# A third score slot from two idle PSUM banks in the w_out stages of a fused attention and squared-ReLU MLP kernel

## The chip, the cores and the metric

The kernel runs on one core of one Trainium2 chip. The metric is device time in microseconds (us). Before the change the median of 11 runs is 370.78 us (370.6 to 372.24).

## What is computed

Attention without a softmax, over 8 batches of 12 heads, 448 tokens and 64 features a head, and then an MLP over the 3584 tokens:

```python
scores = scale * np.matmul(q, k.transpose(0, 1, 3, 2))
attn = np.maximum(scores, 0.0) ** 2 / S
x = np.matmul(attn, v)            # heads side by side: 3584 x 768
g = np.maximum(x @ w_in, 0.0) ** 2    # w_in 768 x 2048
out = g @ w_out                   # w_out 2048 x 768
```

Inputs and outputs are float32 in device memory; on the chip the operands are float16 and the sums float32 in PSUM.

## The kernel before

**Attention.** A unit is four heads of one batch: 24 units, three to a batch. Each unit is cut into 7 tiles of 64 keys. `score` (L252) makes one tile: four matmuls on 64x64 quarters of the array (L262), whose 448 columns go to two PSUM banks, and one ScalarE activation over both banks (L266, relu, 128x896) that writes the tile `at` to SBUF. VectorE then squares `at` in place (L369, queued by `square`). When a unit's seven tiles are squared, `av_unit` (L301) multiplies them with v: 28 quarter-array matmuls (L317) into two banks, and one activation (L323) that writes `xt`.

**A visit** (`visit`, L371) is what the kernel puts between two matmuls of the MLP: a first score tile, then attn x v of a unit if one is due, then a second score tile. Below, S2 is a visit of two tiles, SAS one of two tiles with attn x v between them. Both kinds take their PSUM from a pool of two slots of two banks each (`slot`, L195).

**The MLP** takes the other four banks, which two pools of two banks hold (`big`, handed out by `mm_tile`). Batches 0 and 1 go through `h_group` (plain matmuls, L409), the later ones through `h_period` (L538): 14 products of 6 matmuls, by a Strassen-like scheme that makes 7 block products do the work of 8. The w_out stage (`o_groups`) does the same for two rows of 128 tokens at a time, which is called a group here: seven products, numbered k = 0 to 6 as in its table `products`, of 8 matmuls each (L725). Two banks X and Y collect them. After k = 0, 2, 4 and 5 ScalarE copies X out (`copy`, L627, "m1", "u2", "u3"; at k = 5 L675), and since the later products go on adding to the same bank, k = 4 cannot begin before the copy "u2" of k = 2 is done, nor k = 5 before the copy "u3" of k = 4. VectorE adds the copies to Y (`plus`, L632), and makes the sums of `g` that serve as left operands (`sums`, L594): sum 3 has to be there before k = 4, sum 4 before k = 6. Group n uses the pool n % 2; the first product of group n + 1 stands between k = 4 and k = 5 of group n.

**The order** is written out by hand. The matmuls of the MLP form one list of steps with costs; a clock adds up the costs, and events (visits, prefetches, sums) are put in at steps marked as edges once their time has come. For each pair of batches from the second on, 21 visits of two tiles are spread evenly in time over the w_out stage of the pair before and the first half of its own w_in stage. Between products a visit has to stand on a step with edge set; a k = 5 edge may take one up to 1.6 us early. VectorE's squares wait in queues (`due`, `due_g`), which `fill` and `put` empty by a modelled time; `sums` puts every square that is ready within 0.3 us ahead of the sum. There are four w_out stages, for batch pairs 0 to 3, with 3, 4, 3 and 4 groups; the last has no visits left.

Of the kernel before, what the change touches and what calls it, by code (L numbers as in the profile page):

```python
# [12 lines left out]
FP32 = mybir.dt.float32  # L13
AF = mybir.ActivationFunctionType
# [4 lines left out]
def kernel(  # L19
# [9 lines left out]
    nc = tc.nc  # L29

    B, H, S, D = q.shape
    NT, DM = out.shape
# [11 lines left out]
    J = 7  # L44
    PW = S // J
    NU = 3
    NUN = B * NU
# [7 lines left out]
    SK = 256.0  # L55
    CX = 1.0 / 896.0
# [137 lines left out]
    def slot(dtype, third=False):  # L194
        return (third_p if third else s_p).tile(  # L195
            [P, 2, 2048 // mybir.dt.size(dtype)], dtype, name="slot", tag="slot")
# [54 lines left out]
    now = [0]  # L251
    avt = [None]  # L252

    def score(t, times=1, third=False):
        n, j = divmod(t, J)
        qT, kT = qkt[n]
        ps = slot(FP32, third)
        for hh in list(range(2)) * times:
            r = slice(64 * hh, 64 * hh + 64)
            for hp in range(2):  # L260
                c = slice(64 * hp, 64 * hp + 64)
                nc.tensor.matmul(  # L262
                    ps[c, hh, 0:S], lhsT=kT[r, j, c], rhs=qT[r, :, c],
                    start=True, stop=True)
        at = at_p.tile([P, 2, S], FP16, name="at", tag="at")
        nc.scalar.activation(out=at, in_=ps[:, :, 0:S], func=AF.Relu, scale=SK)  # L266
        ats[t] = at
        seen[t] = now[0]

# [28 lines left out]

    unit = [NU]

    def av_unit():  # L301

        n = unit[0]
        if n == NUN or seen.get(n * J + J - 1, 10 ** 6) >= now[0]:
            return
        unit[0] += 1
        flush(rest=False)
        at_pe[0] += 1.33
        b, u = divmod(n, NU)
        vt = vts[n]  # L310
        ps = slot(FP32)
        for j in range(J):
            at = ats.pop(n * J + j)
            for hp in range(2):
                r = slice(64 * hp, 64 * hp + 64)
                for hh in range(2):
                    nc.tensor.matmul(  # L317
                        ps[64 * hh:64 * hh + 64, hp, 0:S],
                        lhsT=vt[r, hh, j * D:(j + 1) * D], rhs=at[r, hh, :],
                        start=(j == 0), stop=(j == J - 1))  # L320
        if u == 0:
            xts[b] = x_p.tile([P, NM, S], FP16, name="xt", tag="xt")
        nc.scalar.activation(  # L323
            out=xts[b][:, 2 * u:2 * u + 2, :], in_=ps[:, :, 0:S],
            func=AF.Copy, scale=CX)

    def prefetch(m):
        if m >= NUN:
            return
        dma_transpose(m)  # L330
        if m > NPE:
            load_v(m)
        if m + 2 < NUN:
            load_qk(m + 2)
# [7 lines left out]
    at_pe = [0.0]  # L342
    at_ve = [0.0]

    def flush(rest=True):
        for d in (due, due_g) if rest else (due,):
            while d:
                put(d)

    def put(d):  # L350
        ready, cost, fn, _ = d.popleft()
        at_ve[0] = max(at_ve[0], at_pe[0], ready) + cost
        fn()

    def fill(until):
        for d in (due, due_g):
            while d and max(at_ve[0], at_pe[0], d[0][0]) + d[0][1] <= until:
                put(d)

    def now_ve(cost, lag=0.25):  # L360
        at_ve[0] = max(at_ve[0], at_pe[0] + lag) + cost
# [5 lines left out]
    def square(at, lag=0.0):  # L367
        due.append((at_pe[0] + lag, 0.54,
                    lambda: nc.vector.tensor_mul(at, at, at), 0))  # L369

    def visit(tiles):  # L371
        now[0] += 1
        for t in tiles:
            if t % J == 0 and t >= NPE * J:
                prefetch(t // J + 2)
        for t in tiles[:1]:
            score(t)
        av_unit()
        for t in tiles[1:]:
            score(t)  # L380
        at_pe[0] += 0.19 + 0.19 * len(tiles)
        for i, t in enumerate(tiles):
            square(ats[t], 0.6 + 0.85 * i)
# [5 lines left out]
    def mm_tile(i=None, dtype=FP32):  # L389
        if i is None:  # L390
            mm_no[0] += 1
            i = mm_no[0] % len(big)
        return big[i].tile(
            [P, 2048 // mybir.dt.size(dtype)], dtype, name="mm", tag="mm")
# [174 lines left out]
    def tile_of(row):  # L569

        if row in saved:
            return saved[row]
        pr, tb = row
        assert not due_g or due_g[0][3] > 2 * pr + (tb >= 3)
        return gts[pr][:, :, tb * P:(tb + 1) * P]
# [8 lines left out]
    def sums(i, rows, to):  # L584

        a1, a2 = tile_of(rows[0]), tile_of(rows[1])
        x, y = ((a2[:, LO], a2[:, HI]), (to.get(1), a1[:, LO]),
                (a1[:, LO], a2[:, LO]), (a1[:, HI], to.get(2)))[i - 1]
        to[i] = late["s"].tile([P, KH, P], FP16, name=f"s{i}", tag=f"s{i}")
        op = nc.vector.tensor_add if i == 1 else nc.vector.tensor_sub  # L590
        while due and due[0][0] <= max(at_ve[0], at_pe[0]) + 0.3:
            put(due)
        now_ve(0.6)
        op(to[i], x, y)  # L594

    def o_groups(groups, then):
# [5 lines left out]
        def group(n, rows, last):  # L602
# [7 lines left out]
            def needs(k):  # L610

                return max(2 * p + (tb > 2) for p, tb in groups[k]
                           if (p, tb) not in saved)

            def ahead(i, k=n):
                if k < len(groups) and i not in sets[k]:
                    flush_g(needs(k))
                    sums(i, groups[k], sets[k])
# [95 lines left out]
            def step(k, f):  # L714
                acc, fresh, left, right, end = products[k]
                if last and k == 5:
                    acc, fresh = Z, True

                def run():
                    if f == 0 and fresh and k != 3:  # L720
                        acc[:] = [mm_tile((n + (k == 5)) % 2)]
                    if f == 0 and k == 0:
                        ahead(1)
                        ahead(2)
                    nc.tensor.matmul(  # L725
                        acc[0][:, 0:HALF], lhsT=left()[:, f], rhs=right[:, f],
                        start=(fresh and f == 0),
                        stop=(f == KH - 1), skip_group_check=not fresh)
                    if f == KH - 1:
                        end()  # L730
                        if k < 4 and n + 1 < len(groups):
                            some = sum(d[3] <= needs(n + 1) for d in due_g)
                            for _ in range(-(-some // (4 - k))):
                                put(due_g)
                        fill(at_pe[0] + AFTER[k])
                return run

            ls = [[(0.1625, step(k, f), ((2 if k == 5 else True) if f == 0 else False))
                   for f in range(KH)] for k in range(7)]
            if last:  # L740
                ls[6] = [(0.0825, step3(z, f), False) for z in range(2) for f in range(KH)]
# [2 lines left out]
        def pre(i):  # L744
            sums(i, groups[0], sets[0])

        lists = [group(n, rows, rows == LAST) for n, rows in enumerate(groups)]
        for n, ls in enumerate(lists):
            for k in range(7):
# [26 lines left out]
    NB0 = NU * J  # L776
    ps = slot(FP32, True)
# [3 lines left out]
    def s(t, times=2):  # L781
        score(t, times, third=t in THIRD)
# [103 lines left out]
    events = []  # L886
    seq = [[2, 3], 4, [4, 5], [6, 7], [8, 9], 5, [10, 11], [12, 13], [14, 15],
           [16, 17], [18, 19], [20], []]
    for i, ts in enumerate(seq):
        at = (2.5 + i) * T_G  # L890
# [18 lines left out]
    for m in (6, 7):  # L909
        events.append((T_H + (1 + 3 * (m - 6)) * T_G, lambda m=m: prefetch(m)))  # L910
    at0 = T_H + 8 * T_G
    for pr in range(1, B // 2):
        t0 = 2 * NB0 * pr
        end = begin[pr] + T_S - 6.5
        gap = (end - at0) / 21
        for i in range(21):
            ts = [t0 + 2 * i, t0 + 2 * i + 1]
            events.append((at0 + i * gap, lambda ts=ts: visit(ts), True))
        at0 = end
        for i in range(4):  # L920
            events.append((begin[pr] - 6 + i, lambda b=2 * pr, i=i: sums_x(b, i)))
    events.append((at0 + 0.3, lambda: visit([]), True))

    def pre(pr, i):
        def run():
# [29 lines left out]
                steps += periods[b, i0]  # L955
        steps += outs[pr][0]

    clock, last = 0.0, 0.0
    ev = deque(sorted(events, key=lambda e: e[0]))
    for cost, fn, edge in steps:  # L960
        fired = 0
        while ev and edge and ev[0][0] <= clock + (1.6 if edge == 2 and not fired else 1e-3):
            if len(ev[0]) == 3:
                if clock < last + 1.5:
                    break
                last = clock
            ev.popleft()[1]()
            fired += 1
        if fn is not None:
            at_pe[0] += cost  # L970
            fn()
        clock += cost
# [31 lines left out]
```

## Time and profile before

| | |
|---|---|
| median of 11 runs | 370.78 us |
| the profiled execution's own time | 370.75 us |
| its span in the profile | 369.0 us |
| TensorE (PE) busy | 359.9 us, 98% |
| VectorE (DVE), ScalarE (ACT) busy | 265.7 us (72%), 247.5 us (67%) |
| granted TensorE clock | 0.999 |

The span is the profile's first to last instruction; 1.75 us of the execution lie outside of it. "Busy" counts the union of an engine's instructions. A row of the timeline gives start, length, engine, line, operation, destination and source; "x8" means eight instructions merged. "PEld" is the loading of weights, which runs beside the matmuls, and "SPq" a DMA queue. In the chain of waits each row is a stretch of the work that ended last, by what held it.

### The profile page before, as it was taken

The page shows a single profiled execution, that of the slowest core. Times are in us where ns is not written, and L with a number is a line of the kernel's source. Part 1 is how long each engine was busy: PE and PEld are TensorE (multiplying, and loading weights), DVE is VectorE, ACT ScalarE, POOL GpSimd, SP SyncE. Part 2 cuts the span into 40 slices and gives each one's busy share as a digit, 9 for nine tenths or more (in the row PEclk, how much of TensorE's full clock was granted, in tenths as well). Part 3 has the DMA queues.
Part 4 walks back from the last instruction along what each step waited for, and adds up shares of the span by engine and source line. Part 5 has one row for each costly group of instructions (what it writes and reads, how often), then busy time and mean ns, then how long its engine had stood idle before and what let it go on. Part 6 is the DMA issues. An engine that isn't in the chain of part 4 may idle for free.

```text
span 369.0 us, 8720 instructions
## 1 busy us (share of the span) xinstructions
PE 359.9 (98%) x3588; PEld 230.5 (62%) x3588; DVE 265.7 (72%) x470; ACT 247.5 (67%) x371; POOL 107.1 (29%) x128
## 2 busy tenths in 40 slices
PE   8899999999999999999999999999999999999994
PEld 3644445445455778875555588786555689986663
DVE  2997677996777787788585766989766686884442
ACT  3988894787676999876556588887665885532220
POOL 8545521846553155432135045140000000000001
PEclk9999999999999999999999999999999999999999
DMA  7999999999999999998699899692323300003333
GB/s 115 202 204 205 205 204 163 148 162 157 195 164 133 175 98 91 110 111 67 138 161 108 163 155 88 89 115 38 64 73 88 85 3 2 2 0 84 88 90 83
DMA packets 121158, 42.63 MB, mean 116 GB/s; under 512 B 100832, under 2 KB 117760, under 8 KB 121120
## 3 DMA queue, kind: packets, MB, share of 16 engines
q0 software_dynamic: 82912, 23.01, 61.9%
q1 hardware_dynamic: 38048, 18.98, 26.0%
q8 instruction: 28, 0.46, 0.5%
q10 hardware_dynamic: 160, 0.10, 0.1%
q14 instruction: 10, 0.08, 0.1%
HBM read 45.61 MB, written 11.01 MB: 153 GB/s over the span
## 4 chain that ended last, share of the span: by engine, by line
PE 90%; ACT 3%; DVE 3%; issue 1%; DMA 1%; POOLq 0%; POOL 0%; ACTq 0%
PE mm L725 34%; PE mm L538 27%; PE slot L262 10%; PE mm L409 9%; PE slot L317 7%; ACT at L266 3%; DMA q<-in_q_dram 1%; DVE at L297 1%; PE avt L280 1%; PE slot L238 1%; PE mm L238 0%; DVE at L369 0%; PE slot L210 0%; DVE xt L292 0%; ACT u L627 0%
## 5 line engine op out<-in xcount | busy, mean ns | idle before, releaser
L266 ACT ACTIVATE at<-slot 128x896 f16<-128x896 f32 x168 | 145.8, 925 | 22.2 <-PE slot L262 22.2
L369 DVE TENSOR_TENSOR at<-at 128x896 f16<-128x896 f16 x147 | 87.3, 620 | 9.7 <-ACT at L266 9.6
L109 POOL DMA_DIRECT2D qs<-in_q_dram x36 | 35.3, 983 | 114.7 <-DMA qT<-qs 106.9
L725 PEld LDWEIGHTS <-s 128*128 128x128 f16 x440 | 41.5, 98 | 32.7 <-issue 3.6
L262 PE MATMUL slot<-qT,kT 64*64 64x448 f16 x744 | 56.8, 361 | 1.9 <-ACT at L266 1.4
L538 PEld LDWEIGHTS <-w 128*128 128x128 f16 x576 | 54.3, 98 | 5.1 <-issue 4.3
L538 PE MATMUL mm<-xt,w 128*128 128x224 f16 x432 | 48.9, 259 | 0.0
L725 PEld LDWEIGHTS <-g 128*128 128x128 f16 x336 | 31.7, 98 | 24.1 <-issue 4.7
L538 PEld LDWEIGHTS <-ws 128*128 128x128 f16 x432 | 40.3, 98 | 4.7 <-issue 4.7
L632 DVE SCALAR_TENSOR_TENSOR osb<-mm,u 128x384 f32<-128x384 f32 (+1 forms) x30 | 16.2, 543 | 36.4 <-ACT u L627 24.0
L725 PE MATMUL mm<-b,g 128*128 128x384 f16 x224 | 40.7, 326 | 0.0
L725 PE MATMUL mm<-b,s 128*128 128x384 f16 x216 | 39.6, 326 | 0.2 <-DVE s L594 0.2
L409 PE MATMUL mm<-xt,w 128*128 128x448 f16 x192 | 39.8, 354 | 0.0
L725 PE MATMUL mm<-t,s 128*128 128x384 f16 x224 | 39.3, 326 | 0.0
L109 POOL DMA_DIRECT2D ks<-in_k_dram x36 | 35.1, 976 | 8.9 <-DMA b<-in_moe_w_out_dram 5.9
L262 PEld LDWEIGHTS <-kT 64*64 64x64 f16 x744 | 19.0, 104 | 28.7 <-issue 23.3
L561 POOL DMA_DIRECT2D out_dram<-osb x2 | 1.1, 563 | 119.6 <-DVE osb L632 119.6
L627 ACT ACTIVATE u<-mm 128x384 f32<-128x384 f32 x28 | 13.7, 491 | 31.6 <-PE mm L725 27.1
L538 PE MATMUL mm<-x,ws 128*128 128x224 f16 x288 | 34.1, 259 | 0.0
L481 DVE CUSTOM_DVE_ANT_0 g<-mm,m 128x448 f16<-128x448 f32 x36 | 22.4, 624 | 14.9 <-PE mm L538 8.1
L317 PE MATMUL slot<-at,vt 64*64 64x448 f16 x588 | 31.9, 350 | 0.2 <-DVE at L369 0.2
L409 PEld LDWEIGHTS <-w 128*128 128x128 f16 x192 | 17.1, 98 | 19.2 <-issue 5.1
(76 smaller groups left out, 401.0 us busy)
## 6 DMA issues: line engine op xcount, KB each, us to landing
out_dram<-osb SPq DMA_DIRECT2D x52, 192.0 KB, 2.9
vt<-in_v_dram POOLq DMA_DIRECT2D x24, 224.0 KB, 6.1
qs<-in_q_dram POOLq DMA_DIRECT2D x36, 112.0 KB, 4.3
ks<-in_k_dram POOLq DMA_DIRECT2D x36, 112.0 KB, 5.5
w<-in_moe_w_in_dram POOLq DMA_DIRECT2D x8, 384.0 KB, 12.0
b<-in_moe_w_out_dram POOLq DMA_DIRECT2D x4, 768.0 KB, 17.2
q<-in_q_dram POOLq DMA_DIRECT2D x6, 224.0 KB, 7.4
k<-in_k_dram POOLq DMA_DIRECT2D x6, 224.0 KB, 7.8
```

Source lines behind the costliest of these rows:

```text
L109: nc.gpsimd.dma_start(out=t[:, :, hh, :], in_=heads(src, n)[:, hh].rearrange("p (j d) -> p j d", d=D))
L238: nc.tensor.transpose(pss[i][64 * hh:64 * hh + 64, i if n < 4 else 0, j * P:(j + 1) * P], src[:, hh, j * D:(j + 1) * D], ident)
L262: nc.tensor.matmul(ps[c, hh, 0:S], lhsT=kT[r, j, c], rhs=qT[r, :, c], start=True, stop=True)
L266: nc.scalar.activation(out=at, in_=ps[:, :, 0:S], func=AF.Relu, scale=SK)
L317: nc.tensor.matmul(ps[64 * hh:64 * hh + 64, hp, 0:S], lhsT=vt[r, hh, j * D:(j + 1) * D], rhs=at[r, hh, :], start=(j == 0), stop=(j == J - 1))
L369: lambda: nc.vector.tensor_mul(at, at, at), 0))
L409: nc.tensor.matmul(cell[0][:, 0:S], lhsT=w1[f // 4][:, m, (f % 4) * P:(f % 4 + 1) * P], rhs=xts[b][:, m, :], start=(m == 0), stop=(m == NM ...
L481: nc.vector._custom_dve(TENSOR_ADD_SAT, out=gs(s, hi, right), in0=acc(s, y), in1=keep[s, nm], s0=3.4e38, s1=0.0)
L538: nc.tensor.matmul(XY[s][y][:, r * Q:(r + 1) * Q], lhsT=left(k, i0 + 2 * s + r, m), rhs=right(k, m), start=(fresh and r == 0 and m == 0), ...
L627: nc.scalar.activation(out=t, in_=X[0][:, 0:HALF], func=AF.Copy, scale=CO)
L632: nc.vector.scalar_tensor_tensor(out=osb[row][:, c], in0=acc[0][:, 0:cc.stop - cc.start], scalar=CO, in1=keep[nm][:, cc], op0=ALU.mult, op ...
L725: nc.tensor.matmul(acc[0][:, 0:HALF], lhsT=left()[:, f], rhs=right[:, f], start=(fresh and f == 0), stop=(f == KH - 1), skip_group_check=n ...
```

## The change

Visits in w_out stages may have three tiles. The first tile, or attn x v if it is due, then takes two banks of the pool that the current group does not use (`ps=pair[0]`), one bank for each half, and its result is taken out by two activations of 448 columns, one a bank, where the old slot took one of 896. Edges that allow it: the one before k = 2 in every group (three tiles, attn x v or not), and the one before k = 4 in all but the last group of a stage (three tiles, or two without the spare banks if attn x v is due at the next visit). The plan is now a line of tiles against time, which a visit may run ahead of by 1.5 tiles on the named edges and on k = 5. `sums` no longer puts all ready squares first: only those that would be done 0.5 us (sum 3) or 0.9 us (the others) from now on TensorE's clock.

```diff
-    def score(t, times=1, third=False):
+    def score(t, times=1, third=False, ps=None):
...
-        ps = slot(FP32, third)
+        spare = ps is not None
+        ps = slot(FP32, third) if ps is None else [mm_tile(ps), mm_tile(ps)]
...
-        nc.scalar.activation(out=at, in_=ps[:, :, 0:S], func=AF.Relu, scale=SK)
+        if spare:
+            for hh in range(2):
+                nc.scalar.activation(
+                    out=at[:, hh], in_=ps[hh][:, 0:S], func=AF.Relu, scale=SK)
+        else:
+            nc.scalar.activation(out=at, in_=ps[:, :, 0:S], func=AF.Relu, scale=SK)
...
+    def av_due(more=0):
         n = unit[0]
-        if n == NUN or seen.get(n * J + J - 1, 10 ** 6) >= now[0]:
+        return n < NUN and seen.get(n * J + J - 1, 10 ** 6) < now[0] + more
...
-    def visit(tiles):
+    def visit(tiles, spare=None):
...
         for t in tiles[:1]:
-            score(t)
-        av_unit()
+            score(t, ps=None if av_due() else spare)
+        av_unit(spare)
...
-        while due and due[0][0] <= max(at_ve[0], at_pe[0]) + 0.3:
-            put(due)
+        fill(at_pe[0] + (0.5 if i == 3 else 0.9))
         now_ve(0.6)
         op(to[i], x, y)
...
-            ls = [[(0.1625, step(k, f), ((2 if k == 5 else True) if f == 0 else False))
+            free = (n + 1) % 2
+            edges = {2: (free, 3, 3)} if n == len(groups) - 1 else {
+                2: (free, 3, 3), 4: (free, 3, 2)}
+            ls = [[(0.1625, step(k, f),
+                    ((edges.get(k), k == 5) if f == 0 else False))
                    for f in range(KH)] for k in range(7)]
...
+            elif pair is not None and ahead <= 1.5 and clock > last + 1.25:
+                n = min(pair[1 + av_due(1)], NT - tile_no)
+                visit(list(range(tile_no, tile_no + n)), pair[0] if n == 3 else None)
+                tile_no += n
+                last = clock
+            elif ahead <= (1.5 if soon else 0.0) and clock > last + 1.5:
+                n = min(2, NT - tile_no)
+                visit(list(range(tile_no, tile_no + n)))
+                tile_no += n
+                last = clock
```

The number of matmuls, tiles, sums, squares and DMAs is the same as before. `av_unit` with `spare` takes its two banks out with two activations in the same way as `score`.

More of the change, by code (lines that the diff above doesn't have):

```diff
@@ L262, in score @@
                 nc.tensor.matmul(
-                    ps[c, hh, 0:S], lhsT=kT[r, j, c], rhs=qT[r, :, c],
+                    ps[hh][c, 0:S] if spare else ps[c, hh, 0:S],
+                    lhsT=kT[r, j, c], rhs=qT[r, :, c],
                     start=True, stop=True)
         at = at_p.tile([P, 2, S], FP16, name="at", tag="at")
-        nc.scalar.activation(out=at, in_=ps[:, :, 0:S], func=AF.Relu, scale=SK)
+        if spare:
[4 more added lines that the diff above has]
+            nc.scalar.activation(out=at, in_=ps[:, :, 0:S], func=AF.Relu, scale=SK)
         ats[t] = at
@@ L299, with av_unit @@
     unit = [NU]
-    def av_unit():
+    def av_due(more=0):
         n = unit[0]
-        if n == NUN or seen.get(n * J + J - 1, 10 ** 6) >= now[0]:
+        return n < NUN and seen.get(n * J + J - 1, 10 ** 6) < now[0] + more
+    def av_unit(ps=None):
+        if not av_due():
             return
+        n = unit[0]
         unit[0] += 1
@@ L310, in av_unit @@
         vt = vts[n]
-        ps = slot(FP32)
+        spare = ps is not None
+        ps = [mm_tile(ps), mm_tile(ps)] if spare else slot(FP32)
         for j in range(J):
@@ L317, in av_unit @@
                     nc.tensor.matmul(
-                        ps[64 * hh:64 * hh + 64, hp, 0:S],
+                        ps[hp][64 * hh:64 * hh + 64, 0:S] if spare
+                        else ps[64 * hh:64 * hh + 64, hp, 0:S],
                         lhsT=vt[r, hh, j * D:(j + 1) * D], rhs=at[r, hh, :],
@@ L322, in av_unit @@
             xts[b] = x_p.tile([P, NM, S], FP16, name="xt", tag="xt")
+        if spare:
+            for hp in range(2):
+                nc.scalar.activation(
+                    out=xts[b][:, 2 * u + hp], in_=ps[hp][:, 0:S],
+                    func=AF.Copy, scale=CX)
+            return
         nc.scalar.activation(
@@ L911 @@
     at0 = T_H + 8 * T_G
+    plan: list = []
     for pr in range(1, B // 2):
@@ L914 @@
         end = begin[pr] + T_S - 6.5
[L915 to L918, printed above, removed]
+        plan.append((at0, end, t0))
         at0 = end
@@ L921 @@
             events.append((begin[pr] - 6 + i, lambda b=2 * pr, i=i: sums_x(b, i)))
-    events.append((at0 + 0.3, lambda: visit([]), True))
     def pre(pr, i):
@@ L956, with planned @@
         steps += outs[pr][0]
-    clock, last = 0.0, 0.0
+    def planned(t):
+        n = 0.0
+        for a, e, t0 in plan:
+            if t >= a:
+                n = t0 + min(1.0, (t - a) / (e - a)) * 2 * NB0
+        return n
+    clock, last, tile_no = 0.0, 0.0, 2 * NB0
+    NT = NUN * J
     ev = deque(sorted(events, key=lambda e: e[0]))
     for cost, fn, edge in steps:
[L961 to L965, printed above, removed]
-                last = clock
-            ev.popleft()[1]()
-            fired += 1
+        while ev and edge and ev[0][0] <= clock + 1e-3:
+            ev.popleft()[1]()
+        if edge and clock >= plan[0][0]:
+            pair, soon = edge if edge is not True else (None, False)
+            ahead = tile_no - planned(clock)
+            if tile_no == NT:
+                if unit[0] < NUN and clock > last + 1.5:
+                    visit([])
+                    last = clock
[3 more added lines that the diff above has]
+                tile_no += n
+                last = clock
+            elif ahead <= (1.5 if soon else 0.0) and clock > last + 1.5:
[3 more added lines that the diff above has]
+                last = clock
         if fn is not None:
```

## The prediction

> **What bounds the kernel now.** I read the page first, then the chain of waits by line, then the timeline stage by stage. The page:
>
> ```profile
> PE 359.9 (98%) x3588; PEld 230.5 (62%) x3588; DVE 265.7 (72%) x470; ACT 247.5 (67%) x371; POOL 107.1 (29%) x128
> ...
> PE 90%; ACT 3%; DVE 3%; issue 1%; DMA 1%; POOLq 0%; POOL 0%; ACTq 0%
> ```
>
> TensorE is busy 98% of the span and 90% of the chain that ended last. So no other engine is the bound; time can be won only where TensorE loses some between matmuls, or where it waits for ACT or DVE. Both can be read from the timeline of TensorE in the first w_out stage:
>
> ```profile
> 83.08 0.57 PE L262 MATMUL slot<-qT,kT 64*64 64x448 f16 x8
> 83.59 2.77 PE L725 MATMUL mm<-t,s 128*128 128x384 f16 x16
> 86.29 0.57 PE L262 MATMUL slot<-qT,kT 64*64 64x448 f16 x8
> 86.80 1.47 PE L725 MATMUL mm<-b,s 128*128 128x384 f16 x8
> 88.11 1.46 PE L725 MATMUL mm<-b,g 128*128 128x384 f16 x8
> 89.50 0.38 PE L262 MATMUL slot<-qT,kT 64*64 64x448 f16 x4
> ```
>
> Starts are the numbers to use, since ends are modelled. From 86.80 to 88.11 a product takes 1.31 us (1.304 over many). From visit to visit, 83.08 to 86.29, is 3.21. Two products are 2.61. Eight score matmuls are worth 0.37, because four run side by side and a tile adds 0.187 (attn x v, 28 of the same, is 1.32 in the chain). That leaves 3.21 - 2.61 - 0.37 = 0.23 us for going into and out of the quarter-array matmuls. I made this sum for all visits from 67 to 304 us, in w_out and w_in stages, with and without attn x v: 0.22 to 0.25 in nearly all. So **a visit has a fixed price of 0.23 us**, whatever it holds.
>
> Six intervals are longer, by these waits: 0.46 at 113.9, 0.17 at 127.0, 0.36 at 202.0, 0.22 at 285.2, and several of 0.06. Together they are 1.4 us. The cause of the one at 285.2 is in the chain of waits, and it will be needed again:
>
> ```profile
> 285.64 1.60 ACT at L266 x2
> 287.24 0.04 issue
> 287.28 0.50 ACT u L627
> 287.78 0.04 issue
> 287.82 1.46 PE mm L725 x8
> ```
>
> A visit started at 285.20. ACT took its two tiles out from 285.64, and only then, 2.08 us after the visit's start, began the copy u3 of X, which had to end before k = 5 could write X, at 287.82. A short w_in piece of 0.57 us was all that lay between, and TensorE stood for 0.22 us. At 202.0 it is sum 3, late behind squares:
>
> ```profile
> 204.15 0.63 DVE L369 TENSOR_TENSOR at<-at 128x896 f16<-128x896 f16 x1 [0.18 <-ACT at L266]
> 204.69 0.68 DVE L594 TENSOR_TENSOR s<-g 128x1024 f16<-128x1024 f16 x1
> ...
> 205.43 0.34 PE L725 MATMUL mm<-b,s 128*128 128x384 f16 x1 [0.20 <-DVE s L594]
> ```
>
> DVE waited for ACT to make the square's tile, and the sum stood behind it. At 113.9 attn x v waited for a square, behind a `plus` that itself waited for u3.
>
> **Part 1: fewer visits.** I counted the runs of quarter-array matmuls in the two programs' order on TensorE: 88 before, 82 after. All matmuls are the same in number. 6 x 0.23 = **-1.4 us**. The fixed price does not grow with a third tile: the third adds 0.187, as the second does, and these are only moved.
>
> **Part 2: the old waits.** The three in w_out stages, 0.46 + 0.36 + 0.22 = 1.04, all lie in the last group of their stage, where the change rearranges everything. In the new order sum 3 stands ahead of the visit's squares and by the rows' durations is done 0.9 to 2 us before k = 4; the visit before k = 4 that pushed back u3 is gone; and attn x v finds the `plus` further ahead. **-1.0 us.** At 127.0 an attn x v visit followed 24 w_in matmuls after another one with two relus of w_in ahead on ACT; after the change the visits there stand at other places: **-0.2**. If they return, this costs nothing beyond the term. What comes next in these places is part 3.
>
> **Part 3: what the third tile does to ACT.** ACT takes the spare tile out in two halves. No spare eviction exists before; the nearest rows are the relus of w_in, of the same size:
>
> ```profile
> 125.25 1.72 ACT L266 ACTIVATE at<-slot 128x896 f16<-128x896 f32 x2
> 126.84 1.00 ACT L490 ACTIVATE g<-mm 128x448 f16<-128x448 f32 x2
> 127.69 0.97 ACT L266 ACTIVATE at<-slot 128x896 f16<-128x896 f32 x1
> ```
>
> Two full tiles hold ACT from 125.25 to 126.84, 0.80 each (0.82 elsewhere), two halves from 126.84 to 127.69, 0.85. So the third tile puts the next copy back by 0.85 to 0.91 us; I take 0.88, while TensorE gets only 0.19 us more to do. ACT's own extra work, 13 x 0.06 us for thirteen split evictions, is off the path, since ACT is busy 67%.
>
> A rule of the Trainium skill speaks against the change. The page "ScalarE: Activation LUTs", section "Rules for kernel authors", budgets about 0.3 us for each ACTIVATE and 0.83 ns for an element. By it two halves would cost 1.34 us where one full tile costs 1.04, a third tile would delay the copy by 1.34 and the waits of the next paragraph would be near 0.65 us each, 5.2 in all, and the kernel slower than before. The rows above speak against it: 0.85 for two halves beside 0.80 for one tile.
>
> Now the place. A three-tile visit before k = 2 starts at 0. Products go on at 0.69, k = 2 and k = 3 take 2.61, so k = 4 is due at 3.30. ACT starts the copy u2 at 2.08 + 0.88 = 2.96 and k = 4 can start 0.54 later (287.28 to 287.82), at 3.50: a wait of **0.2 us** (0.17 to 0.23). With two tiles it was ready at 2.62, due at 3.11, with 0.5 us to spare, which is why before shows no such wait. Where another visit stands before k = 4 (0.6 us or more) the wait is covered; where none does, it is paid. The same holds for a three-tile visit before k = 4 with no visit before k = 5: u3 at 3.50, k = 5 due at 0.69 + two products = 3.30. In the changed order I count thirteen visits of three tiles. Five are covered; eight are not: in the first stage the one of the last group, in the second stage those of groups 0, 2 and 3 before k = 2 and of group 1 before k = 4, in the third stage group 0 before k = 4 and groups 1 and 2 before k = 2. 8 x 0.19 = **+1.5 us**. From both sides: 0 if ACT gets to the halves early (the first needs only half a tile's matmuls, all four of which run at once, so at most a few hundredths), 8 x 0.46, the longest wait seen, if more is queued: 3.7. I take 1.5, by the nearest row.
>
> **Part 4: the spare banks.** They are those of group n - 1, so the first half waits for the last copy of X there, the second for the `plus` of k = 6 on DVE. This is a new wait, and behind it on TensorE stands everything. In the row of DVE after the attn x v visit at 89.50, the last square ends at 93.76 and the `plus` starts at 94.14. In the new order one more square (0.55) comes before it, and the `plus` of u3 leaves 0.7 us later, since ACT has a third tile ahead of u3. So it ends near 89.50 + 6.0, and the visit comes at 89.50 + 5.83: **+0.2 us**, once. At the other twelve I find the `plus` done 0.1 us or more ahead. Bounds: none (nothing if DVE is 0.2 us earlier), 13 x 0.2 = 2.6.
>
> **Part 5: nothing.** DMA: the transposes of q and k, in the same order on SP, land in 4.5 us (median) and are used two units, some 20 us, later; the first stage draws tiles faster (1.5 us a tile for 1.8) and leaves that cover. No queue of SP or POOL changes its order. If that cover were gone, a unit's first visit would wait; no score matmul waits for a transpose now. The squares moved behind sums 1, 2 and 4 cost nothing as long as attn x v comes later than they do, which is rival 2.
>
> **Sum**, against the profiled execution's 370.75 (span 369.0 and 1.75 outside): 370.75 - 1.4 - 1.0 - 0.2 + 1.5 + 0.2 = **369.9 us**. The median of the runs is 370.78, so both bases are one. A measurement of this kernel can tell about 0.2%, 0.74 us, from no change: 370.04 and below is faster, 371.52 and above slower. The forecast lies 0.1 us beyond the edge.
>
> **Rival 1: the copies do not wait.** If ACT takes halves out sooner than I read, or slack arises elsewhere, the eight waits of part 3 go. Half of them gone: 369.1; all: 368.4. For it: the margin is 0.2 us of 3.5. Against: the same sum gives 287.82 for the wait at 285.2 to the hundredth.
>
> **Rival 2: attn x v waits for squares, and the kernel is slower.** The mechanism is that of 113.9: DVE is in order, the `plus` of u3 waits for ACT, and squares stand behind it. The place is the attn x v visit that follows a three-tile visit holding its unit's last tile: I find four (first stage in groups 0 and 1 and at its end, second stage at its end). In the first of them I get the square done 0.07 us before its matmul, so one more DVE instruction (0.55) decides. Price: the 0.46 us seen once, four times: 369.9 + 1.8 = 371.7; with a further square each, 373.9. It decides from 1.6 us in all, 0.4 a place. Against: in three of the four the sum gives 0.5 us or more to spare, and sums ahead of squares are only two at a time.
>
> **Rival 3: the change doesn't do what it says**, and the two effects cancel: waits of 0.3 instead of 0.19 give 370.8, no change.
>
> **Chances.** The forecast with its own range 369.3 to 370.5: 0.62, half of it below the 0.2% edge. Rival 1: 0.21, faster. Rival 2: 0.12, slower. Rival 3: 0.05. So faster 0.31 + 0.21 = 0.52, within 0.2% 0.31 + 0.05 = 0.36, slower 0.12. The range reaches from 368.6, which leaves out the far third of rival 1 (0.07), to 371.1, which leaves out rival 2 (0.12).
>
> **What would show it.** In the profile after, right: 82 runs of quarter-array matmuls; a "PE mm L746 <- ACT u L648" stretch of some 0.2 us in the chain at eight places; no wait for a sum before k = 4; ACT rows of 448 columns with 0.85 to 0.91 for a pair. Wrong: waits of attn x v for squares on DVE (rival 2), products that start on time after three tiles (rival 1), or a visit's price that is not 0.23 with three tiles, which would undo part 1.

## The result and the profile after

The changed kernel takes **369.62 us** (median of 9 runs, 369.52 to 370.16); the kernel before 370.90 over 35 runs, the 11 of before among them. The ratio is 0.9967, with a 95% interval of 0.9959 to 0.9975: 1.3 us, a third of a per cent, faster. The forecast was 369.9, a change of -0.9 us where -1.3 was measured. The profiled execution took 369.74 us, with a span of 368.0.

The page of the kernel after, engines and chain by engine:

```profile
PE 358.2 (97%) x3588; PEld 232.0 (63%) x3588; DVE 265.5 (72%) x470; ACT 248.6 (68%) x384; POOL 107.5 (29%) x128
...
PE 92%; ACT 2%; DVE 2%; issue 1%; DMA 1%; POOL 0%; POOLq 0%; ACTq 0%
```

The instructions are the same in number but for 13 more on ACT, the split evictions. TensorE still is the bound; its busy time fell by 1.7 us with the same 3588 matmuls. That points the same way as the 1.4 us that six visits cost by the prediction, but it is no measure of them, since the ends of matmuls are modelled.

Where the time went I read as the prediction did: the interval from each visit's first matmul to the next visit's, less its matmuls at their spacing (0.163 us in w_out, 0.0958 and 0.1892 in w_in, 0.0468 in visits). What is left is 0.23 us in an undisturbed interval, and more where TensorE waited. Three of the intervals:

| visit before | left in before | left in after |
|---|---|---|
| k = 5 of the first stage's last group (attn x v; 113.9 / 114.2 us) | 0.70 | 0.24 |
| k = 2 of the second stage's last group (202.0 / 201.2 us) | 0.59 | 0.37 |
| k = 2 of the first stage's last group (three tiles, 108.8 us) | 0.23 (two tiles) | 0.37 |

The first two hold old waits that are gone. The last two hold the new one. Here it is, in the timeline of the kernel after (start, length, engine, line, operation):

```profile
108.82 0.38 PE L263 MATMUL mm<-qT,kT 64*64 64x448 f16 x4
...
109.03 0.55 PE L263 MATMUL slot<-qT,kT 64*64 64x448 f16 x8
109.24 0.98 ACT L270 ACTIVATE at<-mm 128x448 f16<-128x448 f32 x2 [0.17 <-PE mm L263]
...
109.51 2.77 PE L746 MATMUL mm<-t,s 128*128 128x384 f16 x16
110.10 1.74 ACT L273 ACTIVATE at<-slot 128x896 f16<-128x896 f32 x2
110.47 0.69 DVE L615 TENSOR_TENSOR s<-g 128x1024 f16<-128x1024 f16 x1
...
111.69 0.53 ACT L648 ACTIVATE u<-mm 128x384 f32<-128x384 f32 x1
112.27 0.65 PE L746 MATMUL mm<-b,s 128*128 128x384 f16 x3
```

The three tiles come within 0.69 us (108.82 to 109.51). ACT takes the two halves from 109.24 and the two full tiles from 110.10, and begins the copy u2 at 111.69. Two products from 109.51 on would end at 112.12; k = 4 starts at 112.27, just behind the copy. The sum 3 it also needs was begun at 110.47 and done at 111.16, long before. The chain of waits does not show the eight stretches "PE mm L746 <- ACT u L648" that the prediction named as a sign; these waits, 0.13 to 0.14 us each, show in the starts only, and it takes the experiment that holds the third tile to tell what they are.

The runs also differ in their first microseconds, in which q and k arrive: the attn x v visit near 55 us starts between 54.84 and 55.39 us in the ten profiles of this study, and the program up to there is the same but for line numbers. So for small differences I use, beside the medians, the stretch from the start of that visit to the start of the second matmul of the last w_out stage, which has no visits: 272.53 us before, 271.34 after.

### The profile page after: what moved, and what is told of

Same layout as the page of the kernel before. It is cut to its first block, busy times and chain, and to the rows that moved or that the text cites. A ratio compares the mean times of both kernels' runs of the same rounds, so it can differ in the third digit from the quotient of the medians.

```text
span 368.0 us, 8740 instructions
## 1 busy us (share of the span) xinstructions
PE 358.2 (97%) x3588; PEld 232.0 (63%) x3588; DVE 265.5 (72%) x470; ACT 248.6 (68%) x384; POOL 107.5 (29%) x128
## 4 chain that ended last, share of the span: by engine, by line
PE 92%; ACT 2%; DVE 2%; issue 1%; DMA 1%; POOL 0%; POOLq 0%; ACTq 0%
PE mm L746 35%; PE mm L559 27%; PE mm L430 9%; PE slot L263 9%; PE slot L329 7%; ACT at L273 2%; DMA k<-in_k_dram 1%; PE mm L263 1%; DVE at L304 1%; PE avt L287 1%; PE slot L238 1%; PE mm L238 0%; PE mm L329 0%; DVE xt L299 0%; PE mm L728 0%
## 5 line engine op out<-in xcount | busy, mean ns | idle before, releaser
L273 ACT ACTIVATE at<-slot 128x896 f16<-128x896 f32 x156 | 135.5, 928 | 7.4 <-PE slot L263 7.4
L746 PEld LDWEIGHTS <-s 128*128 128x128 f16 x440 | 41.9, 98 | 32.2 <-issue 4.8
L263 PE MATMUL slot<-qT,kT 64*64 64x448 f16 x696 | 53.2, 359 | 1.9 <-ACT at L273 1.4
L746 PEld LDWEIGHTS <-g 128*128 128x128 f16 x336 | 31.9, 98 | 23.5 <-issue 3.8
L746 PE MATMUL mm<-b,g 128*128 128x384 f16 x224 | 40.7, 326 | 0.0
L746 PE MATMUL mm<-b,s 128*128 128x384 f16 x216 | 39.5, 326 | 0.0
L746 PE MATMUL mm<-t,s 128*128 128x384 f16 x224 | 38.8, 326 | 0.0
L263 PEld LDWEIGHTS <-kT 64*64 64x64 f16 x744 | 20.3, 104 | 27.6 <-issue 21.5
L648 ACT ACTIVATE u<-mm 128x384 f32<-128x384 f32 x28 | 14.2, 507 | 30.5 <-PE mm L746 28.4
L329 PE MATMUL slot<-at,vt 64*64 64x448 f16 x560 | 30.1, 349 | 0.0
```

What stands on the lines that cost most here:

```text
L263: nc.tensor.matmul(ps[hh][c, 0:S] if spare else ps[c, hh, 0:S], lhsT=kT[r, j, c], rhs=qT[r, :, c], start=True, stop=True)
L329: nc.tensor.matmul(ps[hp][64 * hh:64 * hh + 64, 0:S] if spare else ps[64 * hh:64 * hh + 64, hp, 0:S], lhsT=vt[r, hh, j * D:(j + 1) * D], r ...
L648: nc.scalar.activation(out=t, in_=X[0][:, 0:HALF], func=AF.Copy, scale=CO)
L746: nc.tensor.matmul(acc[0][:, 0:HALF], lhsT=left()[:, f], rhs=right[:, f], start=(fresh and f == 0), stop=(f == KH - 1), skip_group_check=n ...
```

## The experiments

The theory: six visits fewer at 0.23 us; the old waits go; what is paid for it is that ACT's third tile delays the copies (eight times 0.13) and that one visit waits for a spare bank. The rivals: the order of the sums alone is what helps (A); the third slot alone (B); the new 0.13 us are no wait but a price of three tiles (C). D, E and F stand with the experiments that test them.

**Sums alone.** The kernel before, with one edit:

```diff
-        while due and due[0][0] <= max(at_ve[0], at_pe[0]) + 0.3:
-            put(due)
+        fill(at_pe[0] + (0.5 if i == 3 else 0.9))
```

> The kernel before, with the new rule for sums of g alone (no third slot, old plan, 88 visits). Theory (the gain is 6 visits fewer at 0.23 us, and the old waits in the last group of each w_out stage, less new waits on copies): only the wait for sum 3 at 202.0 goes, 0.36 us, so 370.4 to 370.6 against 370.9, and the waits at 113.9 (0.46) and 285.2 (0.22) stay. Rival A (the order of the sums is what helps, the third slot is only carried along): most of the gain is here already, about 369.8.

Measured: 370.34 us beside 370.70; ratio 0.9996 (0.9986 to 1.0006), which alone does not tell it from no change. (The range of 370.4 to 370.6 was set against 370.9; beside the 370.70 of this experiment the time is 0.36 less, as expected.) The stretch tells: 272.16 us, 0.38 less than before, and the one interval that changed by more than 0.02 us is that of sum 3. In its timeline:

```profile
202.29 0.57 PE L262 MATMUL slot<-qT,kT 64*64 64x448 f16 x8
...
202.88 0.68 DVE L593 TENSOR_TENSOR s<-g 128x1024 f16<-128x1024 f16 x1
...
205.41 0.81 PE L724 MATMUL mm<-b,s 128*128 128x384 f16 x4
```

The sum now starts 0.6 us after the visit, and k = 4 follows on time (3.12 us after the visit; it was 3.47). The waits at 113.9 and 285.2 stayed. Rival A falls.

**Two tiles.** The kernel after, with 2 for 3 at every edge:

```diff
-            edges = {2: (free, 3, 3)} if n == len(groups) - 1 else {
-                2: (free, 3, 3), 4: (free, 3, 2)}
+            edges = {2: (free, 2, 2)} if n == len(groups) - 1 else {
+                2: (free, 2, 2), 4: (free, 2, 2)}
```

> The kernel after, with every three-tile edge made a two-tile edge: new plan and new rule for sums stay, no spare bank is used, 88 visits again. Theory: against after, 6 x 0.23 = 1.4 us more, less the eight waits on copies (8 x 0.13 = 1.1) and the wait on the spare bank (0.15): +0.2, so about 369.8 (369.6 to 370.1). Rival B (the third slot itself carries the whole gain): back to 370.6 or more. Rival A (sums and plan alone): 369.6, the same as after.

Measured: 370.23 us, ratio to before 0.9984 (0.9975 to 0.9992); stretch 272.10. That is 0.6 us over the kernel after (0.8 by the stretch), between theory and rival B and outside the range I gave. The intervals show why: the copies' waits and the bank's wait are gone, 88 visits are back, and five visits before k = 2 have a new wait, four of 0.11 us and one of 0.22. One of them:

```profile
106.95 0.57 PE L263 MATMUL slot<-qT,kT 64*64 64x448 f16 x8
107.38 1.73 ACT L273 ACTIVATE at<-slot 128x896 f16<-128x896 f32 x2 [1.10 <-PE slot L263]
...
108.86 0.69 PE L263 MATMUL slot<-qT,kT 64*64 64x448 f16 x8
```

Two visits stand one product apart. The second tile of the later one needs the slot that ACT empties at 107.38 + 1.73 = 109.11; eight matmuls that take 0.57 us at 106.95 take 0.69 at 108.86. So the third slot is worth more than six visits: in this plan it also removes 4 x 0.11 + 0.22 = 0.66 us of waiting for slots. 1.40 + 0.66 - 1.07 - 0.15 = 0.84 against the 0.76 us between the two stretches.

**Hold the third tile.** The kernel after, with the third tile's relu issued behind the next copy:

```diff
+        elif hold is not None:
+            def relu():
+                nc.scalar.activation(out=at, in_=ps[:, :, 0:S], func=AF.Relu, scale=SK)
+                square(at, hold)
+            held.append(relu)
...
         for t in tiles[1:]:
-            score(t)
+            score(t, hold=1.3 if len(tiles) == 3 and t == tiles[2] else None)
...
                 copy("u2")
+                release()
...
                 copy("u3")
+                release()
```

> The kernel after, with ScalarE's relu of the third tile of a visit issued behind the next copy of X (u2 or u3) rather than ahead of it; its square follows it. Theory: k = 4 and k = 5 wait only for the copy, which stands behind the third tile on ACT; then the eight waits of 0.13 to 0.14 us go, 1.1 in all: 368.5 (368.4 to 368.9). Rival C (these 0.13 us are a price of three tiles on TensorE or of the split eviction, not a wait for the copy): 369.6, no change.

Measured: **368.24 us**, ratio to before 0.9935 (0.9922 to 0.9947); stretch 270.05, 1.29 less than after. The time is just under the range given. All eight intervals are back at 0.22 or 0.23. The same place as above:

```profile
108.58 0.38 PE L269 MATMUL mm<-qT,kT 64*64 64x448 f16 x4
...
109.87 0.92 ACT L284 ACTIVATE at<-slot 128x896 f16<-128x896 f32 x1
...
110.84 0.49 ACT L660 ACTIVATE u<-mm 128x384 f32<-128x384 f32 x1
111.22 0.91 ACT L280 ACTIVATE at<-slot 128x896 f16<-128x896 f32 x1
111.89 1.30 PE L760 MATMUL mm<-b,s 128*128 128x384 f16 x7
```

The copy runs at 110.84, as soon as k = 2 is done, the third relu at 111.22, and k = 4 starts 3.31 us after the visit, where it was 3.45. Rival C falls. Besides the 8 x 0.13 the spare bank's 0.15 went too, which was not expected. The same instructions stand ahead of the `plus` on DVE, but they start earlier: the copy u3 too now goes ahead of a third relu (at 88.49; in after behind it, at 89.27), so its `plus` starts at 89.01, 0.67 us before the attn x v visit at 89.68, where after has it at 89.82, just behind the visit at 89.79. The `plus` that frees the spare bank is then done at 94.91, 0.6 us ahead of the visit at 95.52.

**More visits.** The kernel before, with every third visit of the plan cut in two:

```diff
+            if i % 3 == 1:
+                events.append((at0 + i * gap, lambda ts=ts: visit(ts[:1]), True))
+                events.append((at0 + (i + 0.5) * gap, lambda ts=ts: visit(ts[1:]), True))
+                continue
...
-                if clock < last + 1.5:
+                if clock < last + 1.0:
```

> The kernel before, with every third visit of the plan split into two visits of one tile, half an interval apart: 109 visits in place of 88, the same tiles and matmuls. Theory (a visit has a fixed price of 0.23 us, whatever it holds): 21 x 0.23 = 4.9 us more, 375.7 (375.2 to 376.2). Rival D (the price goes with tiles, or is hidden): 370.9 to 372.

Measured: 376.03 us, ratio 1.0144 (1.0131 to 1.0158); stretch 5.35 us longer. 21 x 0.233 = 4.9; the rest, 0.5 us, is what the new waits, the largest of some 1.0 us at an attn x v visit, come to beyond the old ones that went. A visit of one tile:

```profile
111.21 0.38 PE L262 MATMUL slot<-qT,kT 64*64 64x448 f16 x4
111.52 1.47 PE L725 MATMUL mm<-t,s 128*128 128x384 f16 x8
112.93 0.38 PE L262 MATMUL slot<-qT,kT 64*64 64x448 f16 x4
```

1.72 us from visit to visit, less 1.304 for a product and 0.187 for the tile, is 0.23 again. Rival D falls: the price goes with visits, at one tile, two or three.

**Old sums.** The kernel after, with the edit of the first experiment undone.

> The kernel after, with the old rule for sums (every ready square goes ahead of a sum). Theory: in a three-tile visit the third square is ready some 3.1 us after the visit's start, sum 3 then ends near 4.3, and k = 4 is due at 3.30: about 1.0 us of wait at the eight places with no visit before k = 4 or k = 5 in place of 0.13, and 0.3 at some of the other five: 376 (373 to 378). So the new rule is what allows the third tile. Rival E (the rule removes only the one wait of before, 0.36): 370.0.

Measured: 375.75 us, ratio 1.0129 (1.0115 to 1.0144). The same place once more:

```profile
109.88 0.38 PE L263 MATMUL mm<-qT,kT 64*64 64x448 f16 x4
...
112.93 0.62 DVE L388 TENSOR_TENSOR at<-at 128x896 f16<-128x896 f16 x1 [0.18 <-ACT at L273]
113.47 0.69 DVE L616 TENSOR_TENSOR s<-g 128x1024 f16<-128x1024 f16 x1
...
114.22 0.99 PE L747 MATMUL mm<-b,s 128*128 128x384 f16 x5 [0.87 <-DVE s L616]
```

The third square waits for ACT until 112.93, the sum follows at 113.47, and k = 4 starts 4.34 us after its visit. Six visits cost 1.03 us of wait each, three more 0.23 to 0.53. So the sums' rule is worth 0.4 us alone and 6.1 with the third tile: neither part of the change can be priced without the other. Rival E falls. (The profiled execution is the slowest of the four, 377.18 us; some 0.7 us of it is a visit at 69.05 that waits for a DMA transpose of k, before any of these sums.)

**The bank's wait.** In the kernel after, the visit at 95.6 us takes 3.55 us to the next where its like take 3.40. DVE's two `plus` and TensorE there:

```profile
95.17 0.55 DVE L653 SCALAR_TENSOR_TENSOR osb<-mm,u 128x384 f32<-128x384 f32 x1
95.62 0.53 PE L263 MATMUL mm<-qT,kT 64*64 64x448 f16 x4
95.73 0.56 DVE L653 SCALAR_TENSOR_TENSOR osb<-mm,m 128x384 f32<-128x384 f32 x1
```

The four matmuls into the spare banks take 0.53 us for 0.38: the second half waits for the `plus` of 95.17, which ends at 95.72. The edit moves an instruction of 0.95 us out of DVE's way:

```diff
-        events.append((2 * T_H + 6 + 8 * i, lambda i=i: sums_w1(6 + i)))
+        events.append((2 * T_H + 10.8 + 4.0 * i, lambda i=i: sums_w1(6 + i)))
```

> The kernel after, with two of VectorE's sums of w_in (L185, 0.95 us each) moved: the first from the attn x v visit at 90 us to behind the next visit, the second by about one product. Theory: the 0.15 us at 95.6 are TensorE's wait for the spare bank, which VectorE frees late; with one instruction fewer ahead of the plus that frees it, the interval at that visit is 3.40 and not 3.55 us, the others are as they were. Rival C (a price of three tiles): 3.55 stays. The whole time is 369.6 or 0.1 to 0.2 less, under what one time can tell.

Measured: one time, 369.99 us, with a start 0.3 us later than that of after (55.26 for 54.94); the stretch is 271.18, 0.16 shorter, the interval 3.40, and the eight others 0.36 to 0.37 as they were:

```profile
95.94 0.38 PE L263 MATMUL mm<-qT,kT 64*64 64x448 f16 x4
96.05 0.56 DVE L653 SCALAR_TENSOR_TENSOR osb<-mm,m 128x384 f32<-128x384 f32 x1 [0.74 <-PE mm L746]
96.16 0.55 PE L263 MATMUL slot<-qT,kT 64*64 64x448 f16 x8
```

**Fewer visits still.** Two kernels with the third tile held and `ahead <= 3.0` for `ahead <= 1.5`; the second also allows the edge before k = 4 in last groups.

> The kernel with the third tile held behind the copy (368.24), and visits of w_out stages allowed to run 3 tiles ahead of the plan for 1.5: 15 visits of three tiles, 81 visits in all. Theory: one visit fewer, 0.23 us less: 368.0, if no wait comes back. Rival F (a denser w_out stage overloads ScalarE or VectorE): 368.5 or more.

> As the run before (held third tile, 3 tiles ahead), and the edge before k = 4 is allowed in the last group of a stage too: 16 visits of three tiles, 80 visits. Theory: two visits fewer than with the held tile alone, 0.47 us less: 367.8, but between k = 4 and k = 5 of a last group lie only 0.57 us of w_in work, so that u3, which with the third tile held begins 2.1 us after the visit, is ready at 2.6 when k = 5 is due at 2.6: no wait or a few hundredths. Rival F: 368.5 or more.

Measured: 368.59 us (ratio 0.9939, 0.9927 to 0.9951) and 368.23 (0.9930, 0.9919 to 0.9942); stretches 269.97 and 269.83. Against the held tile alone (270.05) that is 0.08 and 0.22 for an expected 0.23 and 0.47, and neither can be told from it in the times. By its median the first would even fit rival F (368.5 or more; its six times run from 367.89 to 369.57). The traces speak against an overloaded ScalarE or VectorE: no interval got longer but one in the first kernel and two in the second, each by a wait of 0.2 us ahead of k = 5 in a last group. For the second kernel "no wait or a few hundredths" was expected there; that was wrong. In the first of them:

```profile
205.88 0.74 PE L571 MATMUL mm<-xt,w 128*128 128x224 f16 x6
206.14 0.49 ACT L660 ACTIVATE u<-mm 128x384 f32<-128x384 f32 x1 [1.31 <-PE mm L760]
...
206.68 1.46 PE L760 MATMUL mm<-nt,g 128*128 128x384 f16 x8
```

Between k = 4 and k = 5 of a last group stand six w_in matmuls, 0.575 us. The copy u3 starts when k = 4 has left the array and with nothing ahead of it on ACT still ends at 206.63, after 205.88 + 0.575 = 206.46. ACT had stood idle for 1.31 us before it. A visit there used to cover this. Its price is 0.23 us, and it hid 0.2.

## Why the prediction was right

The sign, the size and the steps held; the sum gave 0.3 us too much, and 0.4 us too small a gain, for its base was 370.75 and the median over all runs is 370.90.

- **Part 1, visits:** 82 in place of 88, and 0.23 us each with three tiles as with two: 1.40 us, as predicted.
- **Part 2, old waits:** the three in w_out stages went (0.46, 0.36 and 0.22). The 0.17 us of the w_in stage, which I had counted as gone, came back at another attn x v visit, at 133.5 us. This step failed by 0.2 us: I had said why the old place would be free and not looked at the new ones. (The list of old waits names six intervals; before has seven, and their sum of 1.4 us is right.)
- **Part 3, copies:** exactly the eight places named, and no other. Each measured 0.13 to 0.14 us for a predicted 0.19 (0.17 to 0.23): 1.07 in place of 1.5. The mis-sized part is the third tile's delay of the copy: 2.87 us from visit to copy (108.82 to 111.69) against 2.08 before, 0.79 for the 0.88 I took; k = 4 starts 0.58 us behind the copy's start, not 0.54, which gave 0.04 back. The halves took 0.86 for two, as expected; the two full tiles behind them stood 0.80 apart (1.59 for both), and I had built on the slower row with 0.82. What the prediction held against rival 1, that its sum gives 287.82 to the hundredth, was no test: 2.08 and 0.54 were read at that very place.
- **Part 4, the spare bank:** one wait, at the visit predicted, 0.15 for 0.2.
- **Part 5:** in the profile after no visit's score matmul waited for a transpose. The cover is thin, though: in the trace of the old sums, with the same visits up to there, the one at 69.05 waited 0.66 us for kT.
- **Rival 2** (attn x v behind squares) has left no mark: of the four attn x v intervals after three-tile visits three are at 0.23 to 0.24, the one predicted with 0.07 us to spare among them, and one, at 206.57, is at 0.29. There all 28 attn x v matmuls keep their pace of 0.19 us for four; it is the second score tile, at 208.13, that comes 0.03 us late, just behind the relu at 207.17 that empties its slot at 208.08.

The sum with the measured terms: -1.40 - 1.04 - 0.07 (all waits in w_in stages) + 1.07 + 0.15 = -1.29, for -1.28 in the medians and -1.19 by the stretch. What I had not seen is that the plan and the third slot hang together: with visits one product apart, two slots are too few, which experiment two showed.

The rule of the Trainium skill that spoke against the change ("ScalarE: Activation LUTs", "Rules for kernel authors": about 0.3 us for each ACTIVATE and 0.83 ns for an element) would make two halves cost 0.3 us more than one tile. The page gives this budget for a bias that is an operand of its own; the relus here have a scale and no bias, which the prediction left out. Measured, a half has a row of 0.54 us and a tile one of 0.91, where estimates by the rule are 0.67 and 1.04, and back to back two halves cost 0.86 against 0.80. So less than the rule asks was paid by itself, and less again in a row; the measurement decides.

The page "TensorEngine Tiling (Array Packing)", "Key Properties", says that a change of tiling mode drains TensorE. The 0.23 us a visit, at one, two and three tiles, agree with a cost of that kind. In the starts it is paid going in and coming out: at the visit at 103.70 (after) the first score matmul comes 0.09 us later than the spacing of the product, and the first matmul of the next product 0.09 us later than that of a tile. No run here separates a drain from other costs of the change, such as the loading of weights.

## What to carry to other kernels

Where two kinds of work share an engine, price the change from one to the other apart from the work: here it is 0.23 us a visit, and the lever is the number of visits. Each visit hides something, though, so look at what each queue does in the time that a bigger visit adds: a copy that the next product needs should be issued ahead of work that only has to be done some time, on ACT (the held relu, 1.3 us) as on DVE (the sums, 6.1 us). A part of a change that is worth little by itself (here 0.4 us) can be the one that makes the other part possible.

## What the runs showed of the hardware

- Two activations of 128x448 from PSUM, one behind the other, hold ScalarE 0.86 us from the first start to the start of what follows; one of 128x896 holds it 0.80 in a row, and its own row is 0.91 long. So splitting an eviction in two cost some 0.06 us, at each of the twelve visits of after whose first tile was split.
- The start of a run varies by 0.55 us between ten profiles whose instructions are the same up to there (the attn x v visit near 55 us: 54.84 to 55.39), which is more than several of the effects measured here.
